# A row of D, the placing of 94 VectorE pairs, and the planner's costs in a fused convolution and attention kernel

## The chip, the cores and the metric

The kernel runs on one core of a Trainium2 chip. A core has a matrix engine (TensorE, "PE" in the profile, with its weight loads shown apart as "PEld"), a vector engine (VectorE, "DVE"), an activation engine (ScalarE, "ACT"), a general engine (GpSimd, "POOL") and a queue that only issues transfers (SyncE, "SP"). They run side by side, each through its own list of instructions in a fixed order, and wait for each other through semaphores. The metric is the device time of one launch in microseconds.

## The reference

Two branches work on the same input x (2048 tokens of 640 channels) and are mixed by a gate per token, all in bfloat16:

```python
g = _sigmoid((x * gate_w).sum(-1, keepdims=True))
a = _A_ref(x, A_k, A_v, A_shift_k, A_ssm_k, A_ssm_D)
b = _B_ref(x, B_wq, B_wk, B_wv, B_wo)
return g * a + (1 - g) * b
```

Branch A shifts and mixes k over four taps and multiplies by v, which gives kv. It convolves kv over all 2048 tokens with a filter per channel (written with Fourier transforms of length 4096), adds kv times a factor per channel (ssm_D), and multiplies by x. Branch B is attention with 32 query heads of 20 channels and one shared head of keys and values, softmax over all 2048 keys, and an output projection wo.

## The kernel before, in words

**Attention.** Scores are made with the keys on the partitions. Four heads lie in four strips of 32 partitions (20 channels, a norm row and padding), so four score matmuls of 32 x 512 run side by side in the array. Work is counted in tiles of 128 keys x 512 queries of one head. There are four query blocks I of 512 tokens and eight groups of four heads for each, 32 groups G in all, and 16 key chunks j in each: 2048 tiles. The function `stream` strings the tiles together and cuts them into units of three and two in turn. For a unit, `QK` puts the scores into two or three PSUM banks, `EXP` lets ScalarE write their exponentials (L1194, tiles ETA and ETB), and `PV` multiplies them with the values (L1235), four heads side by side in four column strips of PSUM bank 6. Banks 0 to 2 and 3 and 4 take turns for the scores, and 5 and 7 are left for all else.

**Pairs.** For the chunks that the table `DVE_J` names for a group, two of the four heads are taken off ScalarE. VectorE evaluates their exponentials (`DEXP`): two evacuations of scores (L1224) and three polynomial steps over 1024 elements (L1227, L1228, L1230) give one tile ETd. Their scores "ride", that is they are issued beside a score matmul of another strip. Their PV matmuls come later, as a "late pair" with two matmuls. The slot where the group's other two heads are multiplied leaves two column strips free; this is the slot's "hole" (`m.hole`), and a late pair that fits its columns can be put there. Before the last chunk of a group is multiplied, all its late pairs have to be in.

**Convolution.** Forward transforms of kv and of the filter are matmuls with tables of sines and cosines (`spectra`, L1475), 5 channel blocks of 128 and 8 frequency blocks each. ssm_D enters by one matmul (L1479) for each block of filter frequencies, two for the first block: 128 columns of `Drow`, which is one row, against the first row of a table. VectorE evacuates the spectra, GpSimd multiplies them (`mac`, L1508), and `inverse` (L1541) transforms back. The shift of k is four matmuls with diagonal matrices (`kdiag`, made on VectorE at L1407; L1418).

**Start.** x is loaded in four blocks and transposed on TensorE (`xT`), keys, values and the first queries are projected (`kproj`, `qproj`), and VectorE and ScalarE evacuate the keys into `kT4` (L1063, L1065). GpSimd clears the padded query weights `wq_pad` (`weights2`, L977) and copies the real ones in (L980). The indicator matrices `IndG4` (L914) are small casts on VectorE. `q2` (L1102) sums squared queries for the softmax bound. At the end, finished blocks go through the output projection (`oproj`, L1571; `part`, L1334, and `tail` for the last block).

**What sets the order.** All of this is first a graph of operations with costs, and the class `Scheduler` writes out one order for each engine from it before anything runs. It steps a planned time for each engine and picks, at each step, a ready operation by priority; on TensorE the score, exponential and PV stream goes first, and other matmuls fill the room until the next scores are due. Operations become ready at the planned end of what they need plus a latency (`LATS`, and once attention has started `LATX`, or an entry of `LATM`). A change of kind on TensorE (`MODE`) costs `SWITCH`. `pool_may` says when GpSimd may start beside VectorE[...]: an operation of VectorE marked `port` and one of GpSimd are planned one after the other. Where TensorE has had little work, the plan puts in filler matmuls (L1623 in the stream, L1628 in the start). The planned times order the instructions and do nothing else; the chip runs each list as fast as the semaphores let it.

Of the kernel before, what the change touches and what calls it, by code (L numbers as in the profile page):

```python
# [10 lines left out]
BF16 = dt.bfloat16  # L11
# [9 lines left out]
BEGIN = 0.75  # L21
LATX = 0.12
CEX = 0.0633
LATM = {}
SLA = 0.3
SLB = 0.3
SLACK = 0.05
# [2 lines left out]
FWIN = 3.4  # L30
FGAP = 0.1

MODE = {"qk": "r", "dqk": "r", "pv": "c", "fillc": "c"}
SWITCH = 0.096
PATIENCE = 2.5
ROOM = 0.3
# [1 line left out]
YOUNG = 4.0  # L38
WAITN = 0.5
HOLD = 0.1  # L40
WAITP = 3.0
PVB = 2
NET = 3
NED = 4
# [124 lines left out]
class Scheduler:  # L169
# [111 lines left out]
    def pool_may(self, t):  # L281
        d = self.order["dve"]
        if not d or not HOLD:
            return True
        x = d[-1]
        if not x.port and x.end > t + HOLD:
            return True
        w = [o.ready + (WAITP if o.name != "onorm" else WAITN) for o in self.cand["pool"] if o.ready <= t]
        return bool(w) and t > min(w)

# [35 lines left out]
    def pick_work(self, t):  # L326
# [9 lines left out]
        if self.rows and not (m is not None and m.cont):  # L336
            best = None
            for gr in self.gcand:
                if gr.rides and gr.ready <= t and gr.mms[0].row not in self.rows:
                    b = next((x for x in gr.banks if not self.bank_claimed[x] and not self.bank_busy[x]  # L340
                              and self.bank_ready[x] <= t), None)
                    if b is not None and (best is None or gr.prio < best[0].prio):
                        best = gr, b
            if best is not None:
                gr, b = best
                self.gcand.discard(gr)
                gr.bank = b
                self.bank_busy[b] = True
                gr.mms[0].deps.update(self.bank_last[b])
                return gr.mms[0]  # L350
        if not (m is not None and m.cont):
            for f in self.floats:
                if f.ready <= t and ((self.mode == "c" and t - f.ready > YOUNG) or t - f.ready > OLD or m is None or m.urge):
                    self.floats.remove(f)
                    self.float_left = list(f.tail)
                    self.join(f, t)
                    return f
        elif m.hole:
            for f in self.floats:
                if f.ready <= t and f.cols <= m.hole:  # L360
                    self.floats.remove(f)
                    self.float_left = list(f.tail)
                    for x in f.tail:
                        x.cost = 0.003
                    return f
        if m is not None:
            if m.cont:
# [251 lines left out]
UP = 256.0  # L619

SIDE = (7, 5)
DVE_J = [(), (), (4, 11), (6,), (1, 6, 11), (1, 5, 11, 14), (3, 8, 10), (3, 7, 12), (1, 5, 9, 13), (1, 4, 5, 8, 13), (), (2, 3, 11, 13), (1, 4, 8, 12), (5,), (1, 5, 11), (1, 6, 11), (1, 8, 11), (2, 4, 11, 14), (2, 8, 11, 14), (5, 11), (3, 9), (2, 8, 13), (3, 8), (2, 6, 11, 14), (2, 6, 10, 14), (13,), (1, 4, 7, 10, 13), (2, 7), (1, 7, 9, 13), (1, 5, 12), (1, 6, 11), (2, 4, 10, 14)]
MAC_ALT = ()
SCALE = float(DH) ** -0.5

# [25 lines left out]
class Kernel:  # L651
# [59 lines left out]
    def alloc(self):  # L711
        nc = self.nc
        T = self.T

        def sb(name, shape, dtype):
            T[name] = nc.alloc_sbuf_tensor(name, shape, dtype)
# [58 lines left out]
        sb("rcp", [128, 16], F32)  # L775
        sb("rbc", [128, 512], F32)
        sb("oTn", [128, 512], BF16)
        sb("Drow", [1, D], BF16)
        early0 = [("iota_f", [128, 520], F32), ("iota_s", [128, 128], F32)]
        for i in range(NF // 2):  # L780
            early0 += [(f"tprod{i}", [128, 2, 520], I32)]
# [38 lines left out]
    def loads(self):  # L820
# [2 lines left out]
        wq = aps["B_wq"].rearrange("(p dc) n -> p dc n", dc=NDC)  # L823
        for b in range(NB):
            xl = self.dma(T["xn"][:, 4 * b:4 * b + 4, :], x[:, 4 * b:4 * b + 4, :], writes=[("xn", b)], nbytes=440000,
                          prio=-9 + b, lat=5.3)
            if b == 0:
                self.dma(T["wqst"][:, :, 0:80], wq[:, :, 0:80], writes=[("wqst", 0)], nbytes=300000, prio=-8.5, lat=5.3)
        self.xl = [xl]
        for n, w, pr in (("wkr", "B_wk", -98.8), ("wvr", "B_wv", -98.7)):  # L830
            self.dma(T[n][:, :, :], aps[w].rearrange("(p dc) c -> p dc c", dc=NDC), writes=[n], eng="act",
# [2 lines left out]
                 eng="act", prio=-98.6, lat=5.5)  # L834
        self.dma(T["wqst"][:, :, 80:640], wq[:, :, 80:640], writes=[("wqst", 1)], nbytes=716800, prio=-4,
                 after=self.xl)
        self.dma(T["Drow"][:, :], aps["A_ssm_D"].rearrange("(o d) -> o d", o=1), writes=["Drow"], nbytes=1280, prio=30,
                 after=self.xl)

    def consts(self):  # L840
# [132 lines left out]
    def weights2(self):  # L973
# [1 line left out]
        dst = T["wq_pad"][:, :, :].rearrange("p k (h c) -> p k h c", c=32)  # L975
        src = T["wqst"][:, :, :].rearrange("p k (h c) -> p k h c", c=20)
        self.pool(lambda e: e.memset(T["wq_pad"][:, :, 128:1024].bitcast(I32), 0), (), [("wq_pad", 1)], 2.1, prio=-4,  # L977
                  after=self.crow0 + [self.g.writer["mcol"]])
        for lo, hi in ((4, 8), (8, 16), (16, 24), (24, 32)):
            self.pool(lambda e, lo=lo, hi=hi: e.tensor_copy(dst[:, :, lo:hi, 0:20], src[:, :, lo:hi, :]),  # L980
                      [("wqst", 1)], [("wq_pad", 1)], 0.75 if hi - lo == 4 else 1.5, prio=-4, name="wq_cp")
# [409 lines left out]
    def kshift(self):  # L1391
# [7 lines left out]
        for b in range(NB):  # L1399
# [7 lines left out]
        self.dve(lambda e: e.tensor_tensor(  # L1407
            T["kdiag"][:, :, :, :].rearrange("p c j d -> p (c j) d"), T["ident"][:, :].unsqueeze(1).to_broadcast(sh),
            T["wtap"][:, :, :].rearrange("p c j -> p (c j)").unsqueeze(2).to_broadcast(sh), ALU.mult),
            ["ident", "wtap"], ["kdiag"], c_ps(2560), prio=16, port=True, name="ksh", after=[self.g.writer["kT4", 0, 128]])  # L1410
        for c in range(NDC):
            for q in range(NB):
                pr = 24.0 + 4.0 * c + 0.5 * q
# [37 lines left out]
    def spectra(self, c, fc, base):  # L1451
# [7 lines left out]
        for kind in ("X", "K"):  # L1459
            gr = self.group("spec", base + (0 if kind == "X" else 1))  # L1460
            for comp in range(2):
                for n in range(NF):
# [13 lines left out]
                        self.bank(bk, 256, 256 * comp), lhs, rhs, start=(n == 0), stop=(n == NF - 1)), [tk] + rk,  # L1476
                        c_mm(256))
                    if kind == "K" and n == 0 and (comp == 0 or fc == 0):
                        self.mm(gr, lambda e, bk, lhs=lhs[0:1], comp=comp: e.matmul(  # L1479
                            self.bank(bk, 128, 256 * comp + 128), lhs, T["Drow"][:, CW * c:CW * c + CW], start=False,  # L1480
                            stop=False), [tk, "Drow"], c_mm(128))

# [200 lines left out]
```

## Time and profile before

| | |
|---|---|
| median of 3 runs | 883.04 us (882.44 to 883.62) |
| time of the profiled execution | 883.28 us |
| its span, first to last instruction | 881.5 us |
| ScalarE busy | 860.2 us, 98% |
| TensorE busy | 862.7 us, 98% |
| VectorE busy | 699.8 us, 79% |
| GpSimd busy | 395.2 us, 45% |
| first exponential starts, last ends | 21.09, 871.81 us |
| granted TensorE clock | 1.000 of full |

A group line of the profile names the source line, the engine, the operation, what it writes and reads, the shapes and the count; then the busy sum and the mean duration in ns; then the idle time ahead of it and what ended that. A timeline line begins with the start in us and the duration from the first start to the last end of the merged instructions. Durations can overlap[...]. For TensorE and ScalarE the distance from one start to the next is therefore the better measure of cost. The end of a matmul is modelled.

### The profile page before, as it was taken

The numbers are of one execution on the slowest core, as the hardware profiler recorded it, in microseconds if no ns is written. First come the engines' busy times: TensorE is split into PE (matmuls) and PEld (weight loads), VectorE is DVE, ScalarE is ACT, GpSimd is POOL, SyncE is SP. The second block draws the span as 40 slices with busy tenths as digits, with TensorE's granted clock in tenths as the row PEclk, the third lists the DMA queues.
The fourth block names the chain that finished last, engine by engine and source line by source line (L and its number), as shares of the span: only waits on it lengthen the run. The fifth ranks groups of instructions, "written<-read, shape, count | busy, mean of one in ns | idle before, by whom it ended". The sixth has DMA issues, their size and how long they took to land.

```text
span 881.5 us, 18559 instructions
## 1 busy us (share of the span) xinstructions
PE 862.7 (98%) x8015; PEld 352.1 (40%) x8015; DVE 699.8 (79%) x885; ACT 860.2 (98%) x768; POOL 395.2 (45%) x351
## 2 busy tenths in 40 slices
PE   8999999999999999999999999999999999999997
PEld 5334423433344434444434234443344443233333
DVE  7567998888998887898787988867779869888644
ACT  6999999999999999999999999999999999999995
POOL 3473003476752645574527644545565546620000
PEclk9999999999999999999999999999999999999999
DMA  6900110000100000100000101000100000030211
GB/s 173 227 15 9 31 33 20 14 13 15 43 20 21 19 13 10 43 19 20 13 17 12 44 29 48 20 13 8 43 20 20 13 6 10 13 106 27 65 65 39
DMA packets 49712, 30.69 MB, mean 35 GB/s; under 512 B 32477, under 2 KB 45662, under 8 KB 49630
## 3 DMA queue, kind: packets, MB, share of 16 engines
q1 hardware_dynamic: 48910, 29.13, 12.1%
q8 instruction: 62, 1.02, 0.5%
q10 hardware_dynamic: 720, 0.38, 0.2%
q14 instruction: 20, 0.16, 0.1%
HBM read 17.85 MB, written 6.02 MB: 27 GB/s over the span
## 4 chain that ended last, share of the span: by engine, by line
ACT 56%; PE 41%; DVE 2%; issue 0%; DVEq 0%; POOL 0%; POOLq 0%
ACT ETA L1194 34%; ACT ETB L1194 22%; PE ps L1161 12%; PE ps L1475 10%; PE ps L1235 7%; PE ps L1541 3%; PE ps L1571 2%; PE ps L1623 2%; PE ps L1079 2%; PE ps L1334 1%; PE ps L1628 1%; PE ps L1102 1%; PE ps L992 0%; PE ps L1479 0%; DVE ETd L1230 0%; PE ps L1357 0%
## 5 line engine op out<-in xcount | busy, mean ns | idle before, releaser
L1194 ACT ACTIVATE ETA<-ps 128x1536 bf16<-128x1536 f32 x374 | 577.8, 1545 | 2.8 <-PE ps L1161 1.3
L1194 ACT ACTIVATE ETB<-ps 128x1024 bf16<-128x1024 f32 x373 | 419.9, 1126 | 1.0 <-PE ps L1161 1.0
L1161 PE MATMUL ps<-qT,kT 32*128 32x512 bf16 x2048 | 300.3, 384 | 9.2 <-ACT ETA L1194 4.6
L1508 POOL TENSOR_TENSOR Pp<-X,K 128x512 f32<-128x512 bf16 x120 | 169.7, 1427 | 170.2 <-DVE dX L1228 68.5
L1224 DVE TENSOR_SCALAR dW<-ps 128x512 f32<-128x512 f32 x180 | 123.4, 686 | 62.3 <-PE ps L1161 60.9
L1161 PEld LDWEIGHTS ps<-qT,kT 32*128 32x128 bf16 x2048 | 74.1, 91 | 238.9 <-ACT ETB L1194 113.3
L1235 PE MATMUL ps<-ETA,vaug 128*32 128x512 bf16 x1122 | 154.4, 385 | 0.0
L1235 PE MATMUL ps<-ETB,vaug 128*32 128x512 bf16 x746 | 147.7, 385 | 0.0
L1230 DVE SCALAR_TENSOR_TENSOR ETd<-dX,dW 128x1024 int16<-128x1024 f32 x90 | 128.1, 1423 | 19.7 <-PE ps L1235 19.6
L1228 DVE SCALAR_TENSOR_TENSOR dX<-dX,dW 128x1024 f32<-128x1024 f32 x90 | 137.0, 1522 | 0.5
L1227 DVE SCALAR_TENSOR_TENSOR dX<-dW 128x1024 f32<-128x1024 uint16 x90 | 127.0, 1412 | 1.3
L1508 POOL TENSOR_TENSOR AB<-Pp 128x256 bf16<-128x256 f32 x80 | 73.1, 914 | 65.3 <-DVE dX L1227 21.0
L1475 PE MATMUL ps<-ssm_kT,Tcs 128*128 128x256 bf16 x600 | 93.8, 275 | 0.0
L1541 PE MATMUL ps<-AB,Tcs 128*128 128x256 bf16 x600 | 89.3, 274 | 0.0
L1475 PE MATMUL ps<-kv,Tcs 128*128 128x256 bf16 x600 | 87.3, 275 | 0.1
L1623 PE MATMUL ps<-Tcs,zeros 128*32 128x512 bf16 x1036 | 85.3, 385 | 0.6 <-DVE acc L1297 0.3
L1508 POOL TENSOR_TENSOR Pp<-Pp 128x512 f32<-128x512 f32 x40 | 54.7, 1368 | 47.8 <-DVE ETd L1230 16.1
L1309 POOL TENSOR_TENSOR oTn<-acc,rbc 128x512 bf16<-128x512 f32 x24 | 42.0, 1750 | 61.1 <-DMA rbc<-scr_d 34.2
L1475 PEld LDWEIGHTS ps<-ssm_kT,Tcs 128*128 128x128 bf16 x600 | 49.5, 97 | 39.9 <-issue 31.3
L1541 PEld LDWEIGHTS ps<-AB,Tcs 128*128 128x128 bf16 x600 | 51.8, 98 | 33.7 <-issue 27.2
L1475 PEld LDWEIGHTS ps<-kv,Tcs 128*128 128x128 bf16 x600 | 49.7, 98 | 34.3 <-issue 25.6
L1309 POOL TENSOR_TENSOR oT<-acc,rbc 128x512 bf16<-128x512 f32 x7 | 11.1, 1580 | 77.3 <-DMA rbc<-scr_d 52.1
(131 smaller groups left out, 653.5 us busy)
## 6 DMA issues: line engine op xcount, KB each, us to landing
rbc<-scr_d SPq DMA_DIRECT2D x31, 256.0 KB
scr_o<-oTn SPq DMA_DIRECT2D x24, 128.0 KB, 1.7
xn<-in_A_q_dram SPq DMA_DIRECT2D x4, 640.0 KB, 7.2
kv<-in_A_v_dram SPq DMA_DIRECT2D x4, 640.0 KB, 5.2
out_dram<-outsb SPq DMA_DIRECT2D x14, 160.0 KB, 1.8
oTp<-scr_o SPq DMA_DIRECT2D x12, 160.0 KB, 2.4
wog<-in_B_wo_dram SPq DMA_DIRECT2D x4, 200.0 KB
wo<-in_B_wo_dram SPq DMA_DIRECT2D x4, 200.0 KB, 3.2
```

The source lines that it names most:

```text
L1161: return e.matmul(self.bank(bk), T["kT4"][32 * r:32 * r + 32, 128 * j:128 * j + 128], T[f"qT{G // 8 % 2}"][32 * r:32 * r + 32, G % 8, :], ...
L1194: op("act", lambda e: e.activation(et(n)[:, 0:w], self.ps[:, lo:lo + w], ACT.Exp, scale=SCALE), [("ps", base[n % 2] + k) for k in range(le ...
L1224: self.evac(gr, "dve", lambda e, bk, h=h: e.tensor_scalar(W[:, 512 * h:512 * h + 512], self.bank(bk), SCALE * LOG2E * 128.0, 128.0 * (127 ...
L1227: V(lambda e: e.scalar_tensor_tensor(X[:, :], w, DP, w, ALU.add, ALU.mult), [kW], ["dX"], c_ps(1024), **k)
L1228: V(lambda e: e.scalar_tensor_tensor(X[:, :], X[:, :], DQ, w, ALU.add, ALU.mult), [kW], ["dX"], c_ps(1024), **k)
L1230: V(lambda e: e.scalar_tensor_tensor(T[f"ETd{pe}"][:, :].bitcast(dt.int16), X[:, :], DA, W[:, :], ALU.mult, ALU.add), [kW, "dX"], [("ETd", ...
L1235: return op("pe", lambda e: e.matmul(self.bank(6)[32 * r:32 * r + 32, :], T[va][:, j, :], src, start=(j == 0), stop=(j == NSC - 1), tile_p ...
L1309: self.pool(lambda e: e.tensor_tensor(out, T["acc"][:, :], T["rbc"][:, :], ALU.mult), ["acc", "rbc"], [key], c_pool(512), prio=p, port=Tru ...
L1475: self.mm(gr, lambda e, bk, lhs=lhs, rhs=rhs, comp=comp, n=n: e.matmul(self.bank(bk, 256, 256 * comp), lhs, rhs, start=(n == 0), stop=(n = ...
L1508: f = lambda e: e.tensor_tensor(out, a, b, alu)
L1541: self.mm(gr, lambda e, bk, lhs=lhs, fc=fc, comp=comp, h=h: e.matmul(self.bank(bk, 256, 256 * h), lhs, AB[:, fc, :, comp, :], start=(fc == ...
L1623: sch.filler = [[lambda e, r=r, st=st: e.matmul(self.bank(6)[32 * r:32 * r + 32, :], self.T["zeros"][:, 0:32], self.T["Tcos"][:, 0, 0:512] ...
```

## The change

- `DVE_J` names 94 chunks instead of 90, nearly all placed anew.
- `Drow` has 128 rows. VectorE clears it in the start, the transfer fills row 0, and the matmul takes all 128 rows of the table.
- A late pair put into a hole takes the hole away (`m.hole = None`), so that a slot gets at most one.
- The clearing of `wq_pad` waits for the evacuation of keys 128 to 511; before, it waited for `mcol`, the column that these evacuations add. `kdiag` waits for the last key evacuation; before, for that of keys 128 to 511.
- Planned costs and rules: a VectorE operation that needs another's result is ready 0.3 us after it, 0.12 before; a riding score costs 0.003, 0.04 before; `q2` is a kind of its own; the loads of x have a planned latency of 6.0 us, 5.3 before, and the first piece of the query weights no longer counts towards the planned bandwidth; GpSimd may also start when VectorE has ended its work and no `port` operation is ready within 0.3 us, and otherwise waits up to 6 us, 3 before.

```diff
-LATM = {}
+LATM = {("dve", "dve"): 0.3}
...
-MODE = {"qk": "r", "dqk": "r", "pv": "c", "fillc": "c"}
+MODE = {"qk": "r", "dqk": "r", "pv": "c", "fillc": "c", "q2": "m"}
...
-WAITP = 3.0
+IDLE = 0.3
+WAITP = 6.0
...
+        if x.end <= t and not any(o.port and o.ready <= t + IDLE for o in self.cand["dve"]):
+            return True
         w = [o.ready + (WAITP if o.name != "onorm" else WAITN) for o in self.cand["pool"] if o.ready <= t]
...
                 gr.mms[0].deps.update(self.bank_last[b])
+                gr.mms[0].cost = 0.003
                 return gr.mms[0]
...
                     for x in f.tail:
                         x.cost = 0.003
+                    m.hole = None
                     return f
...
-DVE_J = [(), (), (4, 11), (6,), (1, 6, 11), (1, 5, 11, 14), (3, 8, 10), (3, 7, 12), (1, 5, 9, 13), (1, 4, 5, 8, 13), (), (2, 3, 11, 13), (1, 4, 8, 12), (5,), (1, 5, 11), (1, 6, 11), (1, 8, 11), (2, 4, 11, 14), (2, 8, 11, 14), (5, 11), (3, 9), (2, 8, 13), (3, 8), (2, 6, 11, 14), (2, 6, 10, 14), (13,), (1, 4, 7, 10, 13), (2, 7), (1, 7, 9, 13), (1, 5, 12), (1, 6, 11), (2, 4, 10, 14)]
+DVE_J = [(6,), (), (4, 10), (4, 11), (2, 7, 10), (1, 4, 9, 13), (9,), (2, 7, 12), (3, 8, 13), (2, 6, 10, 14), (3, 9), (1, 4, 8, 12), (1, 2, 7, 10, 13), (8,), (1, 6, 11), (2, 7, 13), (2, 6, 10, 14), (2, 4, 7, 10, 13), (2, 6, 10, 14), (2, 9), (8,), (2, 5, 8, 11, 14), (), (2, 5, 8, 11, 14), (1, 4, 7, 10, 13), (6,), (1, 4, 7, 10, 13), (5,), (1, 4, 8, 12), (2, 5, 10, 11, 14), (1, 10, 11), (2, 8, 13)]
...
-        sb("Drow", [1, D], BF16)
+        sb("Drow", [128, D], BF16)
...
-                          prio=-9 + b, lat=5.3)
+                          prio=-9 + b, lat=6.0)
             if b == 0:
-                self.dma(T["wqst"][:, :, 0:80], wq[:, :, 0:80], writes=[("wqst", 0)], nbytes=300000, prio=-8.5, lat=5.3)
+                self.dma(T["wqst"][:, :, 0:80], wq[:, :, 0:80], writes=[("wqst", 0)], prio=-8.5, lat=5.0)
...
-        self.dma(T["Drow"][:, :], aps["A_ssm_D"].rearrange("(o d) -> o d", o=1), writes=["Drow"], nbytes=1280, prio=30,
+        self.dve(lambda e: e.memset(T["Drow"][:, :], 0.0), (), ["Drow"], 0.4, prio=-990)
+        self.dma(T["Drow"][0:1, :], aps["A_ssm_D"].rearrange("(o d) -> o d", o=1), writes=["Drow"], nbytes=1280, prio=30,
...
-                  after=self.crow0 + [self.g.writer["mcol"]])
+                  after=self.crow0 + [self.g.writer["kT4", 0, 128]])
...
-            ["ident", "wtap"], ["kdiag"], c_ps(2560), prio=16, port=True, name="ksh", after=[self.g.writer["kT4", 0, 128]])
+            ["ident", "wtap"], ["kdiag"], c_ps(2560), prio=16, port=True, name="ksh", after=[self.g.writer["kT4", NB - 1, 0]])
...
-                        self.mm(gr, lambda e, bk, lhs=lhs[0:1], comp=comp: e.matmul(
+                        self.mm(gr, lambda e, bk, lhs=lhs, comp=comp: e.matmul(
```

## The prediction

> **What bounds the kernel now.** I read the page's busy times first, then the groups by line, then ScalarE's starts in order of time, and last the tail.
>
> ```profile
> PE 862.7 (98%) x8015; PEld 352.1 (40%) x8015; DVE 699.8 (79%) x885; ACT 860.2 (98%) x768; POOL 395.2 (45%) x351
> ...
> L1194 ACT ACTIVATE ETA<-ps 128x1536 bf16<-128x1536 f32 x374 | 577.8, 1545 | 2.8 <-PE ps L1161 1.3
> L1194 ACT ACTIVATE ETB<-ps 128x1024 bf16<-128x1024 f32 x373 | 419.9, 1126 | 1.0 <-PE ps L1161 1.0
> ...
> L1623 PE MATMUL ps<-Tcs,zeros 128*32 128x512 bf16 x1036 | 85.3, 385 | 0.6 <-DVE acc L1297 0.3
> ```
>
> ScalarE runs 747 exponentials, of three tiles (ETA) and of two (ETB) in turn. Their durations sum to 997.7 us in a span of 881.5, so they overlap, and only their starts count. TensorE's 98% is no bound over the whole: 1036 of its matmuls are filler. Here are two starts of a quiet stretch and three of a disturbed one (timeline of ScalarE):
>
> ```profile
> 24.46 1.45 ACT L1194 ACTIVATE ETA<-ps 128x1536 bf16<-128x1536 f32 x1
> 25.79 1.03 ACT L1194 ACTIVATE ETB<-ps 128x1024 bf16<-128x1024 f32 x1
> 26.70 1.47 ACT L1194 ACTIVATE ETA<-ps 128x1536 bf16<-128x1536 f32 x1
> ...
> 138.76 0.27 PE L1475 MATMUL ps<-ssm_kT,Tsin 128*128 128x256 bf16 x1
> 138.96 0.22 PE L1479 MATMUL ps<-Drow,Tsin 1*128 1x128 bf16 x1
> 139.12 0.72 PE L1475 MATMUL ps<-ssm_kT,Tsin 128*128 128x256 bf16 x5
> 139.77 0.39 PE L1161 MATMUL ps<-qT,kT 32*128 32x512 bf16 x3
> ...
> 139.10 1.04 ACT L1194 ACTIVATE ETB<-ps 128x1024 bf16<-128x1024 f32 x1
> 140.26 1.45 ACT L1194 ACTIVATE ETA<-ps 128x1536 bf16<-128x1536 f32 x1
> ```
>
> Undisturbed, an ETA takes 1.33 us to the next start and an ETB 0.90 (the medians over all starts are 1.330 and 0.904), so five tiles take 2.234 us and one 0.447. At 139.10 the ETB took 1.16 instead: the scores of the next ETA came 0.25 late, because TensorE was still in a spectrum with a D row. So the stream has a floor, (2048 - 180)/5 x 2.234 = 834.6 us for the 1868 tiles not on VectorE, and ran 850.7 (21.09 to 871.81). **16.1 us are stalls**, 1.1 in the first unit and 14.9 spread over the rest, nearly all after an ETB. The profiled time is 883.28: 21.09 ahead of the stream, 850.7, 9.7 behind it, and 1.8 outside the span; it is 0.24 above the median 883.04.
>
> **The change part by part.**
>
> *94 pairs for 90.* A pair takes two tiles from ScalarE, so eight leave: 8 x 0.447 = **-3.6** (floor 831.0). VectorE gets four pairs of 2 x 0.686 + 1.412 + 1.522 + 1.423 = 5.73 us, 22.9 in all: 722.7 of about 870, hidden on average. Uncovered it costs what the second rival says.
>
> *D row at full height.* From the D row's start to the next matmul I count 157 ns where 128 columns elsewhere take 55 (L1418), and the matmul ahead of it holds 215 instead of 109: 102 + 106 = 208 ns more per D row, 45 times: 9.4 us of TensorE. Here the Trainium skill speaks against the change: TensorE: Matmul & The Clock Gate, Why this matters for your kernels, says that one matmul over 32 rows takes the time of one over 128. The durations agree with it (225 ns against 220), and by it the edit is worth 0. The starts do not: the loss lies on both sides. TensorEngine Tiling (Array Packing), Key Properties, has a rule for that, a change of tiling mode drains the array; a one-row operand uses a different mode. I go by the starts. The gaps between score groups that hold a D row carry 3.05 us of stall (each start against its median, summed); the bounds are 0 (hidden anyway) and -9.4. I take **-3.0**, and **-1.0** of the 2.4 us in spectrum gaps that follow such a gap and start late. The new clearing of Drow (640 bf16 zeros) has no row; the zeros tile's 32 took 72 ns as 16 words, the 512 strided ones at L955 485. 320 words lie between, some 0.35 us; VectorE idles 0.47 us before its first table operation (1.52), which covers it. Uncovered, at most 0.5. The DMA keeps its place in SP's queue (13.27) and waits for nothing unfinished.
>
> *One late pair per hole.* A two-column hole beside an exponential pair's PV takes one late pair at 3 ns. A second runs alone: in 26 such runs the slot took 763 ns instead of 548, so 26 x 0.215 = 5.6 us that the plan counts as nothing. Gaps with late pairs hold 3.2 us of stall. The second pair now goes to another hole or runs where the plan charges it; **-1.5**, between 0 and -3.2.
>
> *Plan costs.* The sums of the squared queries (q2, L1102) get the mode switch that the trace has: 202 ns before one after a spectrum instead of 109, gaps with stall 1.3: **-0.5** (0 to -1.3). Riding scores start 3 ns after their neighbour, so 0.003 for 0.04 is right; nothing. The 0.3 between dependent VectorE operations and POOL's new licence (start when VectorE is idle, otherwise wait up to 6 us) move order. The lone exponential step of 1024 takes 1.21 to 1.23 us, with POOL beside it up to 2.17. Less overlap helps VectorE, longer waiting hurts POOL, which idles 55%. I set the new VectorE load against it: **+0.5**, between -2 and +9.
>
> *Start.* POOL's clearing of the query weights, VectorE's pieces and TensorE's consequence (timelines):
>
> ```profile
> 19.83 1.96 POOL L977 MEMSET wq_pad<- 128x2240 int32 x1
> ...
> 20.13 1.70 DVE L914 CAST IndG<-acol 128x4 bf16<-128x4 f32 x1
> 20.19 1.63 DVE L1063 TENSOR_SCALAR kT<-ps,cols 128x512 bf16<-128x512 f32 x2
> 21.86 0.17 DVE L914 CAST IndG<-acol 128x4 bf16<-128x4 f32 x1
> ...
> 22.66 2.82 DVE L1407 TENSOR_TENSOR kdiag<-ident,wtap 128x2560 bf16<-128x2560 bf16 x1
> ...
> 21.90 1.25 PE L1011 MATMUL ps<-xT,wk 128*128 128x512 bf16 x5 [0.37 <-DVE kT L1063]
> ...
> 23.54 1.02 ACT L1194 ACTIVATE ETB<-ps 128x1024 bf16<-128x1024 f32 x1 [1.00 <-PE ps L1161]
> ```
>
> The first IndG cast takes 1.70 us, until the clearing ends; its sisters take 0.17. Both key evacuations end with it, five projections follow, and the second exponential starts 1.12 late. SBUF — State Buffer, Who interferes with whom, calls the shared VectorE/GpSimd pair an exclusive lock for a whole instruction; so the clearing, moved behind a key evacuation, may catch a later cast instead. By that rule the gain could be 0; by the row, everything the second score needs is ahead of it by then: **-1.0**. Behind it on POOL stand four weight copies (first at 25.55, then already waiting for kdiag) and the table operations. POOL idled 21.8 to 25.5, so it fits; kdiag, now behind the last key evacuation, may push the copies 1.5 us, and their users, the next query tiles evacuated at 33.8, serve a group that starts near 49. The conv behind kdiag shifts likewise, off the stream.
> The planned arrival of x moves from 7.6 to 8.3 us (5.3 to 6.0 of latency), and TensorE gets fillers until then: 0.7 x 0.55/0.2185, two more at 0.216. They end at 8.52 on the chain, while x's first block landed near 5.4: **+0.4** (0 to +0.6).
>
> Sum: -3.6 - 3.0 - 1.0 - 1.5 - 0.5 + 0.5 - 1.0 + 0.4 = -9.7. Span 871.8, profiled time 873.6, from the median **873.3 us**.
>
> **Rivals.**
> 1. *The stalls only move.* A fresh order of 18,000 instructions brings new late scores; ScalarE still loses some 14. Only the pairs and half the start remain: 883.0 - 4 = 879. For it: stalls occur at inverses and output projections too (0.8 and 0.5), with none of the edited causes. Against: most sit beside D rows, late pairs and q2.
> 2. *VectorE becomes the bound (slower).* Groups 21 to 24 get 5, 0, 5, 5 pairs, 16 to 19 get 4, 5, 4, 2: 15 in four groups each, where the densest four had 14. Four such groups last (256 - 30) x 0.447 = 101 us. 15 pairs at 5.73 are 86, other VectorE work (699.8 - 515.5 = 184 over 850, or 22%) adds 22: 108, so 7 us late, twice 14 us, while the late pairs sit in TensorE's order ahead of scores. -9.7 + 14 gives 887. It decides from p = 5.6 us a pair, where 2 x (15p + 22 - 101) reaches 9.7. For it: 22.9 of 24 us busy at 212 to 236. Against: uncontended a pair is 5.06, pairs are computed ahead, spectra can wait.
> 3. *The D row's loss is hidden or stays:* 883.3 - 5.7 = 877.3.
> 4. *Late finish.* POOL waits longer; the last AB ends near 771, inverses start at 783, and from there TensorE is full:
>
> ```profile
> 783.00:836.00 53.00, 52.21 (x465) 21.41 (x464) 42.79 (x52) 53.00 (x48) 3.36 (x3) 1.00 0.23 66
> 836.00:872.00 36.00, 35.84 (x296) 14.18 (x297) 15.44 (x27) 35.76 (x32) 1.27 (x1) 1.00 0.13 46
> ...
> 870.81 1.21 PE ps L1334 x8
> ...
> 872.04 0.56 DVE part L1337
> ```
>
> The last partial projection already ends 0.2 us behind the last exponential (columns of the first two: TensorE, its loads, VectorE, ScalarE, POOL). Fillers after 783 leave 3 us of room. TensorE has some 0.42 free of each us, so 20 us of delay give 20 x 0.42 - 3 = 5.4 us of tail: 878.7.
> 5. *Stalls nearly vanish:* 3 remain, -3.6 - 1.0 - 12 + 0.4 = -16.2: 867.
>
> **How the numbers follow.** The sum's case 0.53 (869 to 877), stalls move 0.15, VectorE bound 0.10, D row worth nothing 0.07, late finish 0.05, stalls vanish 0.10. A measurement cannot tell less than 0.2% (1.8 us) from no change. Slower than 884.8 is the VectorE case, 0.10; within it some 0.03 from the edge of the first and fourth rival; faster 0.87. The range reaches to 866 below and 882.5 above, which leaves out the slower case and a few per cent at each end.
>
> **What would show it.** The exponentials should be 744 or 743; the D row should step 55 ns to the next matmul and 109 before it; the IndG casts all near 0.2 us and the second exponential directly behind the first; no PV slot with two pairs in one hole; the stream's excess over 831 near 8 us. The prediction is wrong if scores wait for late pairs that wait for VectorE, if inverses start after 800, or if the first exponential starts much after 21.5.

## The result and the profile after

| | before | after |
|---|---|---|
| median of 18 runs each | 883.25 us | 876.07 us |
| ratio of the means | | 0.9934 (95%: 0.9917 to 0.9950) |
| profiled execution, its span | 883.28, 881.5 | 876.13, 874.3 |
| first exponential starts, last ends | 21.09, 871.81 | 20.80, 864.93 |
| stream between them | 850.72 | 844.13 |
| of it: floor, stall of the first unit, other stalls, rest of the last exponential | 834.6, 1.12, 14.86, 0.11 | 831.0, 1.71, 11.03, 0.35 |
| *tail*: last exponential to the end of the span | 9.64 | 9.41 |

The change makes the kernel 7.2 us faster by the medians, 0.81%. Four of the 18 runs after took 880.15 to 883.76 us at a mean granted clock of 0.987 to 0.993, against 875.37 to 876.80 us in the other fourteen, and they alone pull the ratio of the means to 0.66%. A stall is here, as in the prediction, the distance of two starts of exponentials less 1.330 us (three tiles) or 0.904 us (two tiles). First the page after, busy times and groups by line (count, then busy sum, mean ns, idle time ahead):

```profile
PE 854.7 (98%) x8054; PEld 351.3 (40%) x8054; DVE 703.0 (80%) x906; ACT 853.4 (98%) x765; POOL 368.8 (42%) x351
...
L1200 ACT ACTIVATE ETA<-ps 128x1536 bf16<-128x1536 f32 x372 | 604.7, 1625 | 2.3 <-PE ps L1167 2.3
L1200 ACT ACTIVATE ETB<-ps 128x1024 bf16<-128x1024 f32 x372 | 447.8, 1204 | 1.6 <-PE ps L1167 1.6
...
L1514 POOL TENSOR_TENSOR Pp<-X,K 128x512 f32<-128x512 bf16 x120 | 154.7, 1301 | 169.4 <-DVE K L1502 56.8
L1230 DVE TENSOR_SCALAR dW<-ps 128x512 f32<-128x512 f32 x188 | 129.0, 687 | 79.1 <-PE ps L1167 78.0
...
L1236 DVE SCALAR_TENSOR_TENSOR ETd<-dX,dW 128x1024 int16<-128x1024 f32 x94 | 133.8, 1423 | 9.7 <-PE ps L1241 9.5
L1233 DVE SCALAR_TENSOR_TENSOR dX<-dW 128x1024 f32<-128x1024 uint16 x94 | 131.3, 1397 | 1.1
L1234 DVE SCALAR_TENSOR_TENSOR dX<-dX,dW 128x1024 f32<-128x1024 f32 x94 | 126.9, 1350 | 0.4
```

There are 744 exponentials, as forecast. The line numbers have moved by 5 or 6. With four pairs more VectorE is only 3.2 us busier (703.0 against 699.8): the four pair groups sum to 521.0 us over 94 pairs, 5.54 a pair, where the prediction had 5.73. GpSimd's product Pp fell from 1427 to 1301 ns. The two engines sit beside each other less: both are busy at once for 268 us, before for 303.

A D row in TensorE's timeline after:

```profile
502.00 0.27 PE L1481 MATMUL ps<-ssm_kT,Tcs 128*128 128x256 bf16 x1
502.11 0.22 PE L1485 MATMUL ps<-Drow,Tcs 128*128 128x128 bf16 x1
502.17 0.38 PE L1481 MATMUL ps<-ssm_kT,Tcs 128*128 128x256 bf16 x2
502.48 0.39 PE L1167 MATMUL ps<-qT,kT 32*128 32x512 bf16 x3
```

The step to it, from start to start, is 0.11 us and the step from it 0.06 (before, 0.20 and 0.16 in the lines that the prediction showed). Over all 45, the medians are 120 and 56 ns, where they were 215 and 157; the duration stayed (219 ns for 225).

The start after (timelines of GpSimd, VectorE, TensorE and ScalarE):

```profile
21.31 1.97 POOL L983 MEMSET wq_pad<- 128x2240 int32 x1 [1.80 <-DVE IndG L920]
...
21.09 0.16 DVE L920 CAST IndG<-acol 128x4 bf16<-128x4 f32 x1
21.94 1.36 DVE L920 CAST IndG<-acol 128x4 bf16<-128x4 f32 x1
22.35 0.95 DVE L1069 TENSOR_SCALAR kT<-ps,cols 128x512 bf16<-128x512 f32 x1
...
23.38 0.60 PE L1167 MATMUL ps<-qT,kT 32*128 32x512 bf16 x5 [0.30 <-DVE Tcs L932]
...
20.80 1.45 ACT L1200 ACTIVATE ETA<-ps 128x1536 bf16<-128x1536 f32 x1 [0.92 <-PE ps L1167]
23.84 1.02 ACT L1200 ACTIVATE ETB<-ps 128x1024 bf16<-128x1024 f32 x1 [1.59 <-PE ps L1167]
```

The clearing now runs from 21.31 to 23.28. The first two casts are free of it; the third (21.94) takes 1.36 us and ends with it, and so does the last key evacuation queued behind. The fourth cast follows at 23.33. The second exponential is 1.71 us late instead of 1.12. Thirty microseconds later lies the only other stall above 0.5 us, at the first unit of the second group (VectorE with the first of its query evacuations and the norm row, the transfer queue of SP, TensorE, ScalarE):

```profile
36.80 0.74 DVE L1096 TENSOR_SCALAR qT<-ps,cols 128x512 bf16<-128x512 f32 x1
47.56 0.68 DVE L1114 TENSOR_SCALAR cr<-ps 8x512 int16<-8x512 int32 x1 [0.25 <-PE ps L1108]
...
48.26 0.60 SPq L679 DMA_DIRECT2D qT<-cr  x1
...
50.62 0.60 PE L1167 MATMUL ps<-qT,kT 32*128 32x512 bf16 x5
...
48.66 1.06 ACT L1200 ACTIVATE ETB<-ps 128x1024 bf16<-128x1024 f32 x1
51.11 1.45 ACT L1200 ACTIVATE ETA<-ps 128x1536 bf16<-128x1536 f32 x1 [1.40 <-PE ps L1167]
```

The scores of that group need the norm row of their queries, `cr`, which a transfer puts into qT. It was issued at 44.41 before, at 48.26 now; the scores follow 2.36 us later, and the exponential is 1.55 late.

The end after, as the chain that ended last gives it, and the first inverse of the last channel block after and before (timelines of TensorE):

```profile
864.01 0.93 ACT ETB L1200
864.94 0.04 issue
864.98 0.62 PE ps L1241 x8
865.60 0.92 PE ps L1363 x6
...
766.41 0.28 PE L1547 MATMUL ps<-AB,Tcs 128*128 128x256 bf16 x1
...
780.55 0.28 PE L1541 MATMUL ps<-AB,Tcs 128*128 128x256 bf16 x1
```

Behind the last exponential come only its own PV and the last block's projection. The inverses of the last block start at 766.4, 14 us earlier than before (780.5). The interval from there to the last exponential's end is called the *lead* below: 98.5 us, before 91.3.

### The profile page after: what moved, and what is told of

It is laid out like the page before. It is cut to its first block, busy times and chain, and to the rows that moved or that the text cites. A ratio compares the mean times of both kernels' runs of the same rounds, so it can differ in the third digit from the quotient of the medians.

```text
span 874.3 us, 18639 instructions
## 1 busy us (share of the span) xinstructions
PE 854.7 (98%) x8054; PEld 351.3 (40%) x8054; DVE 703.0 (80%) x906; ACT 853.4 (98%) x765; POOL 368.8 (42%) x351
## 4 chain that ended last, share of the span: by engine, by line
ACT 93%; PE 6%; DVE 1%; DVEq 0%; POOL 0%; issue 0%; POOLq 0%
ACT ETA L1200 55%; ACT ETB L1200 38%; PE ps L1167 1%; PE ps L1634 1%; PE ps L998 1%; PE ps L1241 1%; PE ps L1085 1%; PE ps L1424 1%; PE ps L1629 0%; PE ps L1017 0%; PE ps L1363 0%; PE ps L1025 0%; DVE outsb L1387 0%; PE ps L1372 0%; DVE IndG L920 0%; PE ps L1108 0%
## 5 line engine op out<-in xcount | busy, mean ns | idle before, releaser
L1200 ACT ACTIVATE ETA<-ps 128x1536 bf16<-128x1536 f32 x372 | 604.7, 1625 | 2.3 <-PE ps L1167 2.3
L1200 ACT ACTIVATE ETB<-ps 128x1024 bf16<-128x1024 f32 x372 | 447.8, 1204 | 1.6 <-PE ps L1167 1.6
L1514 POOL TENSOR_TENSOR Pp<-X,K 128x512 f32<-128x512 bf16 x120 | 154.7, 1301 | 169.4 <-DVE K L1502 56.8
L1230 DVE TENSOR_SCALAR dW<-ps 128x512 f32<-128x512 f32 x188 | 129.0, 687 | 79.1 <-PE ps L1167 78.0
L1236 DVE SCALAR_TENSOR_TENSOR ETd<-dX,dW 128x1024 int16<-128x1024 f32 x94 | 133.8, 1423 | 9.7 <-PE ps L1241 9.5
L1233 DVE SCALAR_TENSOR_TENSOR dX<-dW 128x1024 f32<-128x1024 uint16 x94 | 131.3, 1397 | 1.1
L1234 DVE SCALAR_TENSOR_TENSOR dX<-dX,dW 128x1024 f32<-128x1024 f32 x94 | 126.9, 1350 | 0.4
L1514 POOL TENSOR_TENSOR AB<-Pp 128x256 bf16<-128x256 f32 x80 | 63.2, 790 | 74.4 <-DVE dX L1234 29.8
L1481 PE MATMUL ps<-ssm_kT,Tcs 128*128 128x256 bf16 x600 | 89.4, 274 | 0.0
L1315 POOL TENSOR_TENSOR oTn<-acc,rbc 128x512 bf16<-128x512 f32 x24 | 38.2, 1593 | 76.3 <-DVE dX L1234 32.8
```

What stands on the lines that cost most here:

```text
L1200: op("act", lambda e: e.activation(et(n)[:, 0:w], self.ps[:, lo:lo + w], ACT.Exp, scale=SCALE), [("ps", base[n % 2] + k) for k in range(le ...
L1230: self.evac(gr, "dve", lambda e, bk, h=h: e.tensor_scalar(W[:, 512 * h:512 * h + 512], self.bank(bk), SCALE * LOG2E * 128.0, 128.0 * (127 ...
L1233: V(lambda e: e.scalar_tensor_tensor(X[:, :], w, DP, w, ALU.add, ALU.mult), [kW], ["dX"], c_ps(1024), **k)
L1234: V(lambda e: e.scalar_tensor_tensor(X[:, :], X[:, :], DQ, w, ALU.add, ALU.mult), [kW], ["dX"], c_ps(1024), **k)
L1236: V(lambda e: e.scalar_tensor_tensor(T[f"ETd{pe}"][:, :].bitcast(dt.int16), X[:, :], DA, W[:, :], ALU.mult, ALU.add), [kW, "dX"], [("ETd", ...
L1315: self.pool(lambda e: e.tensor_tensor(out, T["acc"][:, :], T["rbc"][:, :], ALU.mult), ["acc", "rbc"], [key], c_pool(512), prio=p, port=Tru ...
```

## The experiments

Every kernel here computes the whole reference. The order of all engines is planned from costs and dependencies, so most edits move thousands of instructions; two could be made that leave the order as it was.

**D row alone, on the kernel before** (e_drow).

```diff
-        sb("Drow", [1, D], BF16)
+        sb("Drow", [128, D], BF16)
+        self.dve(lambda e: e.memset(T["Drow"][:, :], 0.0), (), ["Drow"], 0.4, prio=-990)
-        ... T["Drow"][:, :]     -> T["Drow"][0:1, :]   (transfer)
-        ... lhs=lhs[0:1]        -> lhs=lhs             (matmul)
```

> The kernel before with the D row as a full-height matmul and nothing else: every engine's order stays, VectorE alone clears Drow once more in the start. Theory (the loss lies in the drain on both sides of a one-row matmul): the start-to-start after a D row falls from 157 to about 55 ns and the one ahead of it from 215 to about 109; the stall in gaps that hold a D row falls from 3.05 us to under 0.5, some of what follows late goes too, and the time falls by 3 to 5 us, to 878 to 880. Rival (a matmul over one row takes the time of one over 128): nothing changes, 883.2. Rival (TensorE has room, the loss is hidden): the starts change as the theory says, but the time falls by less than 1 us.

Measured: 880.22, ratio 0.9968 (0.9956 to 0.9981). Apart from the one new clearing, each engine has the order of before. TensorE's timeline at the D row that the prediction showed:

```profile
138.04 0.27 PE L1475 MATMUL ps<-ssm_kT,Tsin 128*128 128x256 bf16 x1
138.15 0.22 PE L1479 MATMUL ps<-Drow,Tsin 128*128 128x128 bf16 x1
138.21 0.71 PE L1475 MATMUL ps<-ssm_kT,Tsin 128*128 128x256 bf16 x5
138.85 0.39 PE L1161 MATMUL ps<-qT,kT 32*128 32x512 bf16 x3
```

From the spectrum matmul ahead of it to the next score group it takes 0.81 us; it took 1.01 (138.76 to 139.77). The gaps with a D row lose 2.63 us of stall (3.05 to 0.42), the gaps directly behind them 1.24 (1.54 to 0.30), and elsewhere 1.0 comes back: the stream is 2.83 shorter. So the mechanism is shown by this run, at 0.7 of the size that the prediction gave it.

Is it the single row that costs, or the change of height beside it? In three of the 45 places of before, the D row stands directly behind a score matmul of 32 rows:

```profile
147.34 0.39 PE L1161 MATMUL ps<-qT,kT 32*128 32x512 bf16 x3
147.35 0.22 PE L1479 MATMUL ps<-Drow,Tcs 1*128 1x128 bf16 x1
147.67 0.83 PE L1475 MATMUL ps<-ssm_kT,Tcs 128*128 128x256 bf16 x6
```

There the step to it is 4 ns and the step from it 314; in e_drow they are 317 and 66, so the two steps together are no longer with one row. And the step from a spectrum matmul to a score of 32 rows is 205 ns in before, e_drow and after, where one to the next spectrum matmul is 109. So each change between few rows and full height costs some 0.1 us, and between two spectrum matmuls the D row brought two of them.

**D row undone, on the kernel after** (e_no_drow): the matmul goes back to `lhs[0:1]` and row 0 of Drow, with planned cost and order as after.

> The kernel after with the one-row matmul put back and the same order on every engine. Theory: 45 times 208 ns of TensorE come back that the plan doesn't know, in the same places: 3 to 6 us slower than the kernel after, 879 to 882. Rival (the new order has room where the D rows lie): within 1.5 us of the kernel after, 876 to 877.5.

Measured: 877.95, ratio 0.9946 (0.9934 to 0.9959), 1.9 us above after. The D-row gaps carry 2.88 of stall again (0.39 after), and the stream is 1.47 longer. The edit is worth 1.5 to 2.8 us of stream, depending on the order that it stands in.

**Clearing where it was** (e_gate_back):

```diff
-                  after=self.crow0 + [self.g.writer["kT4", 0, 128]])
+                  after=self.crow0 + [self.g.writer["mcol"]])
```

> The kernel after with the clearing of the query weights on POOL released by mcol again, as in the kernel before. Theory (the clearing's move holds an IndG cast and a key evacuation, and makes the second group's queries late): the 1.7 us ahead of the second exponential fall to about 1.1, and the 1.55 us stall at 51 us goes: about 2 us faster than the kernel after, 874. Rival (the stall at 51 us comes from the pair that group 0 now has and from kdiag's move, not from the clearing): 0.6 us faster at most, and the stall at 51 us stays.

Measured: 888.35, ratio 1.0060 (1.0048 to 1.0073). VectorE's timeline shows the collision of before again, and ScalarE's the stall of the second group:

```profile
20.14 1.72 DVE L920 CAST IndG<-acol 128x4 bf16<-128x4 f32 x1
20.21 1.66 DVE L1069 TENSOR_SCALAR kT<-ps,cols 128x512 bf16<-128x512 f32 x2
...
53.18 1.45 ACT L1200 ACTIVATE ETA<-ps 128x1536 bf16<-128x1536 f32 x1 [2.79 <-PE ps L1167]
```

The collision costs 2.06 at the first unit here, and the second group's stall is 3.08, larger than with the clearing moved. The query-weight copies behind the clearing are early in this kernel (22.93 to 30.9; after 26.31 to 33.5), so late copies are not what makes that stall. The stream is 2.1 us longer than after; the other 10 of the 12 us are at the end: inverses at 796.2, lead 71.2, tail 19.28. A gate that touches one instruction at 20 us has changed when the last channel block is convolved.

**Clearing early** (e_early_clear): out of reach of the casts.

```diff
-                  after=self.crow0 + [self.g.writer["kT4", 0, 128]])
+                  after=[self.g.writer["tprod", 3]])
...
+                      after=self.crow0 + [self.g.writer["kT4", 0, 128]])   (the four copies)
...
-                     0.15, **k)      (IndG casts)
+                     0.15, prio=-1)
```

> The kernel after with the clearing released by the last table operation of VectorE (near 8.5 us, where POOL is idle), the IndG casts no longer held back to the keys' time, and the weight copies released by the key evacuation. Theory: no cast meets the clearing, the second exponential follows the first directly (1.7 us less), and the second group's queries are ready before 49 us (1.5 us less): about 3 us faster than the kernel after, 873. Rival (the weight copies then meet the key evacuations or kdiag, or a new order brings new stalls): 875 to 878.

Measured: 877.27, ratio 0.9933 (0.9919 to 0.9947), no gain: the median is 1.2 us above after's and the stream 1.0 longer. The clearing ran at 12.4 and the first-unit stall went from 1.71 to 0.58. But the norm row is issued at 49.31, 1.05 later than after, and the second group's stall went from 1.55 to 3.47. The transfer sets when that group starts, so what the stream wins ahead of it is waited for there.

**No pair in group 0** (e_pair01): `DVE_J[0] = ()`, `DVE_J[1] = (8,)`, again 94 pairs.

> The kernel after with group 0's pair (chunk 6) moved to group 1 (chunk 8), still 94 pairs. Theory (the pair in group 0 holds VectorE while the second group's queries are made, and the stall at 51 us is its price): that stall of 1.55 us goes and the last exponential ends 1.5 us sooner, near 863.4. Rival for the stall (the clearing's move): it stays. What the new order does to the end of the convolution is open: in it POOL's multiplications come later, and if the inverses begin after 785 us the time behind the last exponential grows from 9.4 to 15 us or more, so that the whole is slower than the kernel after.

Measured: 884.40, ratio 1.0016 (1.0007 to 1.0026). The stall of the second group is 0.31, although its norm row is issued at 47.79, only half a microsecond earlier than after; the stream is the shortest of all with 94 pairs, 842.93, and the last exponential ends at 863.30. Yet the time is 8.3 us longer: inverses at 787.4, lead 75.9, tail 18.68.

**One late pair per hole, alone, on the kernel before** (e_hole): `m.hole = None`.

> The kernel before with at most one late pair in a hole and nothing else. Theory: the 24 slots with two pairs go, the stalls in gaps with late pairs fall from 3.2 to about 1.7 us, the last exponential ends 1.5 us sooner. Rival (late finish): all the orders are new, with the old table of pairs, and the convolution may end later; each us that the inverses begin after 785 adds some 0.4 us behind the last exponential. 880 to 882 by the first, over 885 by the second.

Measured: 887.62, ratio 1.0051 (1.0036 to 1.0066). Slots with six PV matmuls and just two late pairs fall from 24 to 2, stalls in gaps with late pairs from 3.19 to 1.85, and the stream is 2.97 us shorter. The end takes back more than that: inverses at 794.7 (780.5 before), lead 73.7, tail 17.09.

**The table alone** (e_pairs: before with the 94 pairs) **and everything but the table** (e_pairs_back: after with the 90 pairs).

> The kernel before with the new table of 94 pairs and nothing else. Theory (the pairs are worth 3.6 us of ScalarE wherever they are put): the stream is 3.6 us shorter and the time 879 to 880. Rival (the table fits the new planning rules alone): under the old rules POOL, which waits up to 3 us and not for an idle VectorE, ends its multiplications later than 785 us, and the time behind the last exponential grows by more than 3.6 us: 884 to 890. Rival (VectorE becomes the bound): scores wait for late pairs in groups 16 to 24, and the stream itself is no shorter.

> The kernel after with the old table of 90 pairs. Theory: the floor is 3.6 us longer, the stall at 51 us is gone (no pair in group 0, 1.5), so the last exponential ends near 867. If the inverses of the last block begin 91 us ahead of it, 878; if the old table ends the convolution later under the new rules (inverses less than 85 us ahead), 881 to 886.

| | rules of before | rules of after |
|---|---|---|
| 90 pairs of before | 883.25 | 882.14, 0.9990 (0.9981 to 1.0000) |
| 94 pairs of after | 893.87, 1.0125 (1.0110 to 1.0140) | 876.07, 0.9934 (0.9917 to 0.9950) |

The two effects don't add: -1.1, at the edge of what can be told from no change, and +10.6 make -7.2. In e_pairs the stream is only 1.35 shorter than before for a floor 3.57 lower (new stalls of 1.63 at the second group and 0.77 at 28.67, where the granted clock is 0.50), the lead is 56.7 and the tail 22.45, in e_pairs_back 89.1 and 12.67, while its stream is 4.15 us shorter than before.

**GpSimd's rules undone** (e_pool_back): after with `WAITP = 3.0` and without the rule on an idle VectorE.

> The kernel after with POOL's old rules (wait up to 3 us, no start because VectorE is idle). Theory: a step of VectorE over 1024 elements goes from 1.39 back to about 1.45 us and POOL's last multiplication from 765 to over 780 us, so that the inverses and output projections no longer fit under the stream: 880 to 887. Rival (the rules only change the order a little): 875 to 877.

Measured: 886.51, ratio 1.0045 (1.0029 to 1.0061). The stream is as long as after (844.35), and 9.8 us of the loss are in the tail. The mean of the polynomial steps goes from 1390 to 1432 ns, VectorE's busy time from 703.0 to 714.3, and the last product AB from 764.6 to 791.0. Its chain, in order of time, and its first inverse:

```profile
864.10 2.01 PE ps L1575 x13
866.12 0.57 PE ps L1239 x8
...
870.58 5.09 PE ps L1338 x36
875.66 0.03 issue
875.69 0.56 DVE part L1341
...
876.30 0.99 PE ps L1361 x6
...
794.47 0.28 PE L1545 MATMUL ps<-AB,Tcs 128*128 128x256 bf16 x1
```

The last exponential ends at 865.86. Output projections (L1575) are still running then, and 36 partial projections (L1338) for 5.09 us follow; in the chain of after the last block's projection (L1363, here L1361) starts 0.67 us behind the last exponential, here 10.4.

How much of this the rules themselves cost is not shown. GpSimd's last products need the last block's spectra, and these already come late. TensorE's timeline with the last spectrum matmuls of after, e_pool_back and e_gate_back, then the busy times of the last two:

```profile
736.72 0.82 PE L1481 MATMUL ps<-ssm_kT,Tcs 128*128 128x256 bf16 x6
...
755.57 1.05 PE L1479 MATMUL ps<-ssm_kT,Tcs 128*128 128x256 bf16 x8
...
769.66 0.72 PE L1481 MATMUL ps<-ssm_kT,Tcs 128*128 128x256 bf16 x5
...
PE 856.2 (97%) x8118; PEld 354.8 (40%) x8138; DVE 714.3 (81%) x906; ACT 853.5 (96%) x765; POOL 389.9 (44%) x351
...
PE 859.8 (97%) x8106; PEld 352.8 (40%) x8106; DVE 701.3 (79%) x906; ACT 853.7 (96%) x765; POOL 368.7 (42%) x351
```

The last of these matmuls starts at 737.3 after, at 756.3 in e_pool_back and at 770.1 in e_gate_back. So 19.0 of the 28.1 us by which e_pool_back's inverses are later than after's are there before GpSimd has its last input. And e_gate_back keeps the new rules, its VectorE and GpSimd are no busier than after's, and its inverses are later still. Less time of the two engines beside each other is therefore not enough for an early end, and the 10.4 us are the price of the rules and of the new order together.

**Two other tables.** e_table has after's code and 98 pairs, none in groups 0 and 1, chosen by the planner's own end time; e_best is e_early_clear with 100 pairs, found in the same manner.

```diff
-DVE_J = [(6,), (), (4, 10), (4, 11), ...   (94 pairs)
+DVE_J = [(), (), (3, 4, 10), (5, 11), (2, 6, 10), (1, 7, 9, 12), (8,), (2, 7, 10, 12), ...   (e_table: 98)
+DVE_J = [(6,), (), (4, 11), (4, 10), (2, 5, 9), (1, 4, 9, 13), (9,), (2, 7, 13), ...   (e_best: 100)
```

> The kernel after with another table of pairs and nothing else: 98 pairs, none in groups 0 and 1, chosen by searching for a table whose order ends early by the planner's own times. Theory (what decides is the stream's floor plus its stalls, so long as the inverses of the last block begin some 91 us ahead of the last exponential): four pairs more give 3.6 us, the stall at 51 us goes (1.5): the last exponential ends near 860, the time behind it stays under 11 us, in all 870 to 872. Rival (VectorE becomes the bound with 98 pairs): the stalls outside the start grow from 9.5 to over 13 us: 874 or more. Rival (late finish): the last block's inverses begin less than 85 us ahead of the last exponential, 875 to 880.

> The early clearing together with a table of 100 pairs, found in the same manner. Six pairs more than after give 5.4 us and the start 1.1; the stall at 51 us stays and is as long as with the early clearing alone (3.5 instead of 1.55): 871 to 873 by the theory. Rival (VectorE becomes the bound with 100 pairs): stalls outside the start over 14 us, 876 or more.

e_table: 874.24, ratio 0.9903 (0.9889 to 0.9918), less gain than expected. Its floor is 3.6 us lower than after's, its stream 2.46 lower, with a new stall of 1.40 at 375 us, and its lead of 91.9 leaves a tail of 10.73. The stall comes with a low clock: the stretch around it shows a granted clock of 0.60 (third figure from the end), and spectrum matmuls in it stand 0.21 us apart instead of 0.109.

```profile
371.50:375.80 4.30, 4.30 (x28) 1.77 (x20) 3.56 (x5) 3.26 (x4) 3.06 (x3) 0.60 0.05 8
```

e_best: **872.32, ratio 0.9884 (0.9868 to 0.9901)**, faster than both kernels. Page, then timelines of ScalarE and GpSimd:

```profile
PE 847.8 (97%) x7955; PEld 348.6 (40%) x7955; DVE 739.9 (85%) x935; ACT 848.5 (97%) x761; POOL 360.2 (41%) x351
```

```profile
21.35 1.45 ACT L1201 ACTIVATE ETA<-ps 128x1536 bf16<-128x1536 f32 x1 [0.92 <-PE ps L1168]
23.25 1.02 ACT L1201 ACTIVATE ETB<-ps 128x1024 bf16<-128x1024 f32 x1 [0.46 <-PE ps L1168]
...
12.81 1.97 POOL L983 MEMSET wq_pad<- 128x2240 int32 x1 [5.28 <-DVE tprod L900]
```

The clearing lies at 12.81, and the second exponential is 0.58 late. The stream is 839.52, 4.6 shorter than after for a floor that is 5.4 lower; lead 111.4, tail 9.43. VectorE at 85% with 100 pairs adds no stall in the sum: outside the first unit and the second group's 3.47 us, the stalls are 9.5 us, as after.

**What sets the tail.** All kernels in one table (us), with the start of the last spectrum matmul:

| kernel | last spectrum | inverses start | lead | tail |
|---|---|---|---|---|
| e_pairs | 782.6 | 812.7 | 56.7 | 22.45 |
| e_gate_back | 770.1 | 796.2 | 71.2 | 19.28 |
| e_pool_back | 756.3 | 794.5 | 71.4 | 19.24 |
| e_hole | 766.4 | 794.7 | 73.7 | 17.09 |
| e_pair01 | 758.1 | 787.4 | 75.9 | 18.68 |
| e_pairs_back | 751.1 | 778.1 | 89.1 | 12.67 |
| before | 743.1 | 780.5 | 91.3 | 9.64 |
| e_drow | 739.4 | 777.0 | 91.3 | 9.65 |
| e_table | 743.1 | 770.8 | 91.9 | 10.73 |
| after | 737.3 | 766.4 | 98.5 | 9.41 |
| e_no_drow | 738.6 | 767.5 | 98.5 | 9.40 |
| e_early_clear | 745.3 | 765.3 | 100.8 | 9.42 |
| e_best | 724.6 | 749.5 | 111.4 | 9.43 |

When the last block's inverses start, 128 inverse matmuls are left at steps of 0.109 us, 120 output and 48 partial projections at 0.136, 37 us of TensorE. From 91 us of lead on, the tail is 9.4 to 9.7 us (e_table 10.7), which no earlier start removes. So, as an estimate, the stream leaves these matmuls about 37 / 91 = 0.40 of each microsecond. Below, a missing microsecond costs about that 0.4: by 9.4 + 0.4 x (91.3 - lead), the tails lie between 0.8 under (e_pairs) and 3.1 over (e_pair01).

The six kernels with a longer tail are also the six whose last spectrum starts at 751 us or later; in the others it starts at 745 or earlier. And they hold more filler matmuls than the others (1084 to 1156, against 924 to 1072), so their TensorE did not lack room for the spectra. Why the plan holds the spectra back in these six is open.

## Why the prediction was right, and where it was not

The time, 876.07, is 2.8 above the 873.3 and inside the likeliest case's range, but it lies halfway between the sum and the first rival's 879. The span fell by 7.12 instead of 9.7: 0.30 ahead of the stream, 6.59 in it and 0.23 behind. In the stream, the floor gave 3.57 and the stalls outside the start and the second group 5.4 (14.9 to 9.5); those two places took back 0.6 and 1.55, and the end of the last exponential 0.2. That nothing was lost behind the stream is luck: the sum has no term for it, and six of the seven orders that one edit changed, without a search for a table, lose 3 to 13 us there.

- *94 pairs, -3.6.* Right in the floor, with 744 exponentials; under the old rules (e_pairs) the same pairs shorten the stream by 1.35 only. VectorE's 5.73 a pair was 5.54.
- *D row, -3.0 and -1.0.* The mechanism was right: what the one-row matmul lost on both sides decided, not its duration. As a whole the term was too large: 2.83 alone, 1.47 as the last part. In e_drow the D-row gaps gave 2.63 and the gaps behind them 1.24, near the two numbers, but 1.0 came back elsewhere, which the sum had no term for. The new clearing took 325 ns and the first table operation still starts at 1.52: hidden, as said.
- *One late pair per hole, -1.5, and q2, -0.5.* The late-pair gaps lost 1.34 in e_hole and 2.06 in after, the q2 gaps 1.04 in after. But the hole rule alone makes the kernel 4.4 us slower, by a late finish that the step did not ask about. q2 and the riding cost were not run alone.
- *New VectorE load against GpSimd's rules, +0.5.* This step failed in its sign. "longer waiting hurts POOL" is not borne out by the two rules together: in the eight kernels with the new rules GpSimd is busy for 360 to 371 us, in the five with the old ones for 390 to 404, and undoing both on after makes the last AB 26 us later (764.6, 791.0) and costs 10.4 us. The two were not undone apart, and part of the 10.4 us is the new order, since e_gate_back is as late with the new rules. The row that spoke for them was in the prediction (1.21 us alone, up to 2.17 beside GpSimd), but it was weighed on the average. Taken with the other terms, the spread stalls came out as summed (-5.4 against -5.5).
- *Clearing moved, -1.0.* This step failed: it became +0.6. "everything the second score needs is ahead of it by then" is wrong: VectorE's order puts the third IndG cast and the last key evacuation behind the gate. The rule that was weighed there (the Trainium skill, SBUF — State Buffer, Who interferes with whom: an exclusive lock for a whole instruction) gave the other reading, that a later cast is caught, and the third cast's 1.36 us is that. e_early_clear, which moves both the clearing and the casts, gains 1.13 us at this place.
- *"their users, next query tiles evacuated at 33.8, serve a group that starts near 49".* The slack was claimed from the evacuation and the group's start, without the norm-row transfer between them. It is issued at 43.7 to 44.4 in before, e_drow and e_hole, and at 47.8 to 50.2 in the other ten. The three of those ten without a pair in group 0 (e_pair01, e_pairs_back, e_table) stall 0.2 to 0.3 there, the seven with it 1.5 to 3.5. The pair takes 0.9 us of exponentials out of group 0, so group 1 is due sooner, and in after and e_gate_back its steps run on VectorE beside the query evacuations. In e_pair01, without it, the transfer is 0.47 earlier and the stall 1.24 less. The prediction priced pairs by the group's load on VectorE alone. Why the planner puts the query projections later in the ten is open.
- *x latency and fillers, +0.4.* Not to be read: the first exponential starts 0.30 earlier, but between before and e_drow, which have the same order, it moved 0.72.

**The signs.** The number of exponentials and the steps of the D row came as said. The casts, the second exponential and the stream's excess did not: the excess over 831 is 13.1, not "near 8", and the sum's own terms give 16.1 - 6.5 = 9.6. Slots with six PV matmuls and just two late pairs fell from 24 to 2.

**The rivals.** The first (the stalls only move) came in part. In gaps with a D row, a late pair, q2 or a spectrum the stalls fell by 6.7 us in all, and in the other gaps they rose by 2.8, of which 1.55 at the second group. The second (VectorE the bound) did not come, not even with 100 pairs; its count of pairs in four groups is one short on both sides (15 before, in groups 6 to 9; 16 after, in groups 15 to 18). Against the fifth stand stalls of 12.7 us and not 3. The third is near in time (877.3, though 883.3 - 5.7 is 877.6), but its reason is refuted by e_drow and e_no_drow. The fourth is the one that the runs met six times: not in after, whose inverses start 14 us earlier, but in e_hole, e_pairs, e_pool_back, e_gate_back, e_pair01 and, by 3 us, e_pairs_back. Its place was right, and so was the tail's mechanism; in those kernels the spectra too are late, and not GpSimd's waiting alone. Two of its readings of before are off: the last AB ends at 779.6 and not 771, and the inverses start at 780.5 and not 783. And its price was too low. "Fillers after 783 leave 3 us of room" does not hold: before, at a lead of 91.3, stood at the edge, and e_pairs_back pays 3.0 us for a lead 2.2 shorter. By 0.42 a microsecond less 3, a start 14.2 us later (e_hole) should cost 3.0 us; it cost 7.5. Counted by the lead, which is 17.6 us shorter since the stream ends earlier too, and with no room, 0.42 x 17.6 = 7.4. And the threshold "if inverses start after 800" was too late: four kernels lose 7 us or more with inverses between 787 and 797.

## What to carry to other kernels

Where one planned order carries everything, undoing one edit measures the new order as well as the edit: compare orders first, and believe those runs whose order stayed. Read off how much work of another engine is left when its last input arrives, and how much room the bounding stream leaves for it; here 37 us of TensorE at 0.40 a microsecond, so an edit that shortens the stream by 3 us and delays that input by 14 loses. A slack counts only when each transfer on the way is in it.

## What was unexpected in the hardware

- A clearing on GpSimd of 1.97 us holds a VectorE cast of four elements a row, which takes 0.16 us elsewhere, for 1.35 to 1.82 us in eleven of the kernels, until it ends; with the clearing at 12.81 or 12.4 us, no cast is held and the first-unit stall falls to 0.58.
- A matmul of one row between two of full height lasts no longer (225 ns, at full height 219) and yet costs 0.20 us of steps: 215 + 157 ns start to start around it, 120 + 56 at full height. Directly behind a score of 32 rows it costs nothing (4 + 314 ns, at full height 317 + 66).
- With GpSimd started more in VectorE's pauses, VectorE does the same 94 pairs and all else in 703.0 instead of 714.3 us, and GpSimd its work in 368.8 instead of 389.9: both engines gain. Whether the kernel gains depends on the order: e_gate_back has 701.3 and 368.7 us and is slower than e_pool_back.
